# Joining neighbouring filter spectra by accumulating DMA instead of VectorE adds, in a gated mix of a long convolution and a token-mixing MLP

## The chip, the cores and the metric

One core of one Trainium2 chip runs the whole kernel. The metric is device time in microseconds (us). Before the change three runs gave 226.09, 227.66 and 223.95 us; the median is 226.09 us.

## The reference

Sequence length S is 2048, width D is 640, the MLP's hidden width F is 1536, batch 1. Cut to what matters:

```
g = sigmoid((q * gate_w).sum(-1))
k_shift[t] = sum_j k[t - 3 + j] * shift_k[:, j]          # 4 taps, causal
kv = k_shift * v
y  = causal convolution of kv with ssm_k, length S, per column   # rfft/irfft of 2S
a  = q * (y + kv * ssm_D)
h  = layernorm(q);  u = gelu(w1^T h + b1);  b = w2^T u + b2       # mixes tokens
out = g * a + (1 - g) * b
```

## The kernel before

**Engines and their order.** Every operation is handed to a planner (`_Plan`, class at line 322) with an engine, a guessed cost, a priority, and the regions that it reads and writes. The planner simulates the engines and writes out one fixed order for each of PE (matmul), ACT, DVE and POOL and for the two queues that issue transfers, SP and POOL. At run time every engine goes through its list in order; a wait for data or for a buffer holds up all that stands behind it on that engine. PSUM is four slots of 1024 columns (`pp0` to `pp3`).

**The convolution by blocks.** The sequence is cut into P = 4 blocks of 512 rows. Filter block i (`wnat`, transposed on PE into `wT`, its even part split into `ee`) is transformed by matmuls with cosine and sine tables (`TFc`, `TFs`, `TN`) into a spectrum `W0` to `W3` of nine rows of 640 columns on 128 partitions: real parts of four frequency groups f = 0 to 3 (rows 0 to 3), a row 4 for the real part's Nyquist term, and imaginary parts (rows 5 to 8). `w_freq` copies each PSUM tile into `W` on ACT with a scale.

`w_comb(i)` then joins neighbours, from i = 3 down to 1: in groups 2 and 3 `W_i += W_(i-1)`, in groups 0 and 1 `W_i -= W_(i-1)`. `w_nyq(i)` copies row 3 into row 4, then one element row of row 8 into row 4, both by DMA on SP, and zeroes partition 0 of row 8 (`memset`, on POOL). It does this for all four spectra, W0 among them.

**The input blocks.** For block j, four tiles of the key with its four taps (`k4`, 128 x 2560) are loaded by SP, multiplied by the taps on DVE (`k<-k,shkb`), added up over the taps by PE with `ident` or `flip`, copied to `kvb` by ACT, and multiplied by `v` on DVE. A DVE split (`es`) and 32 matmuls with `AFc` and `AFs` give the spectrum `A_j`, copied to SBUF by ACT. There is one `kvb` and one `es` buffer.

**Products and inverses.** For output block m, `pair(j, m)` multiplies `A_j` with `W_(m-j)` on DVE, for j = 0 to m, and adds up into `Z` (two buffers; `tT` is the scratch). `inverse(m)` turns `Z` back by 32 matmuls with the table `TI`; `epilogue` copies the results (`qb`, `pb`), flips by PE, scales by the gate on ACT into `cg`, and combines on DVE with the MLP's result `o` and with `xe`, then stores by SP. For the last m the products are split by frequency group.

**The MLP.** `h` comes from a layernorm on DVE; the first product (`pp<-h,w`, 384 matmuls) and the second (`pp<-gT,w`, 384) fill PE wherever nothing else is ready. Weights come by DMA on POOL's queue (`w1_0` to `w1_2`, `w2_0`, `w2_1`), each load waiting for PE to have done with the old tile. The gate's row sums (`xg`) use DVE and ACT.

Of the kernel before, what the change touches and what calls it, by code (L numbers as in the profile page):

```python
# [8 lines left out]
BF16 = mybir.dt.bfloat16  # L9
F32 = mybir.dt.float32  # L10
I32 = mybir.dt.int32
ACT = mybir.ActivationFunctionType
ALU = mybir.AluOpType
# [4 lines left out]
class _Tracker:  # L18
# [227 lines left out]
    def dma(self, stream, out_ap, in_ap, semname, noncontig=False, accum=False):  # L246
        reads = [in_ap]
        writes = [out_ap]
        acc = self.pre(stream, reads, writes)
        engobj = self.eng[stream]  # L250
        sem = self.dma_sems[semname]
        if accum:
            ins = engobj.dma_start(out_ap, in_ap, accum_op=ALU.add)
        elif noncontig:
            with self.nc.allow_non_contiguous_dma(reason="tiny"):
                ins = engobj.dma_start(out_ap, in_ap)
        else:
            ins = engobj.dma_start(out_ap, in_ap)  # L258
        ins.then_inc(sem, 16)
        self.dma_cnt[semname] += 16  # L260
        v = self.dma_cnt[semname]
        self.dma_hist[(semname, v)] = dict(self.known[stream])
        src = ("dma", semname, v)
        for reg, mode in acc:
            self.add_record(reg, mode, src)
        return v
# [250 lines left out]
def _build(nc, A_q, A_k, A_v, A_shift_k, A_ssm_k, A_ssm_D, B_x, B_w1, B_b1, B_w2, B_b2, gate_w, out):  # L517
    Bsz, S, D = A_q.shape
# [4 lines left out]
    n = S // P  # L523
    N2 = 2 * n
# [4 lines left out]
    HD = D // 2  # L529
# [3 lines left out]
    with ExitStack() as es:  # L533
# [3 lines left out]
        T = _Tracker(nc, clk)  # L537
# [5 lines left out]
        plan = _Plan(T, 4)  # L543
# [4 lines left out]
        def buf(name, shape, dtype, t0, t1):  # L548
            spec.append((name, list(shape), dtype, t0, t1))

        END = 999
# [33 lines left out]
        buf("AFc", [128, 1024], BF16, 0, 90)  # L585
        buf("AFs", [128, 1024], BF16, 0, 90)
        buf("TI", [128, 2, 4, n // 2], BF16, 0, END)
        buf("h", [128, NT, D], BF16, 0, 80)
        groups = [[0], [1]] + [[t, t + 1] for t in range(2, NT, 2)]
        for i in range(2):  # L590
# [50 lines left out]
        for name, shape, dtype, t0, t1 in spec:  # L641
            size = mybir.dt.size(dtype)
# [31 lines left out]
        def tt(out_, in0, in1, op, pr, eng="DVE"):  # L674
            c = 0.07 + nel(out_) / 1920.0 if eng == "DVE" else 0.3 + nel(out_) / 500.0
            return vop(eng, c, lambda e: e.tensor_tensor(out_, in0, in1, op), [in0, in1], [out_], pr)  # L676

        def ts(out_, in0, s1, s2, op0, op1, pr, eng="DVE", cost=None):
            c = cost if cost is not None else (0.1 + nel(out_) / 1500.0 if eng == "DVE" else 0.4 + nel(out_) / 900.0)

            def f(e):
                if s2 is None:
                    return e.tensor_scalar(out_, in0, s1, None, op0=op0)
                return e.tensor_scalar(out_, in0, s1, s2, op0=op0, op1=op1)

            rr = [in0] + [a for a in (s1, s2) if isinstance(a, bass.AP)]
            return vop(eng, c, f, rr, [out_], pr)
# [5 lines left out]
        def memset(ap, val, pr, eng="POOL"):  # L693
            return vop(eng, 0.3 + nel(ap) / 2000.0, lambda e: e.memset(ap, val), [], [ap], pr)

        def act(out_, in_, func, pr, bias=None, scale=None, accum=None, ps=(), after=()):
            kw = {}
            rr = [in_]
            k = 0
            if bias is not None:  # L700
                kw["bias"] = bias
                if isinstance(bias, bass.AP):
                    rr.append(bias)
                    k += 1
            if scale is not None:
                kw["scale"] = scale
                if isinstance(scale, bass.AP):
                    rr.append(scale)
                    k += 1
            ww = [out_]  # L710
            if accum is not None:
                kw["accum_out"] = accum
                ww.append(accum)
            c = 0.17 + nel(out_) / 1150.0 + 0.09 * k + (0.2 if accum is not None else 0)

            def f(e):
                src = in_() if callable(in_) else in_
                return e.activation(out_, src, func, **kw)  # L718

            return vop("ACT", c, f, rr, ww, pr, ps=ps, after=after)  # L720

        def dma(out_ap, in_ap, semname, pr, stream="SP", noncontig=False):
            if semname not in T.dma_sems:
                T.add_dma_sem(semname, es.enter_context(nc.semaphore(f"d_{semname}")))
            tot = mybir.dt.size(out_ap.dtype)
            for st, ct in list(out_ap.ap):
                tot *= ct

            def emit():
                T.dma(stream, out_ap, in_ap, semname, noncontig=noncontig)  # L730

            return plan.add(stream, 1.2 if stream == "POOL" else 0.5, emit, [in_ap], [out_ap], pr, dma=max(tot, 20000) / 1e6)

        def pe(pslist, mms, pr, after=()):
            reads = []
# [11 lines left out]
        def two(p_):  # L747
            return lambda: pp[p_.slot][:, :].rearrange("p (c f) -> p c f", c=2)[:, :, 0:HD]
# [4 lines left out]
        def h2(ap):  # L753
            return ap.rearrange("p (c f) -> p c f", c=2)

        b = bufs
# [11 lines left out]
        c_pi, c_hp, c_mh, c_w, c_w0, c_mn, c_mn2 = (cst[:, i:i + 1] for i in range(7))  # L768
# [42 lines left out]
        TFc, TFs, AFc, AFs, TI = b["TFc"], b["TFs"], b["AFc"], b["AFs"], b["TI"]  # L811
# [72 lines left out]
        for gi, g in enumerate(groups):  # L884
            xs = b[f"xs{g[0] // 8}"][:, g[0] % 8:g[-1] % 8 + 1, :]
            gn = len(g)
            pr = 1.0 + g[0] * 0.08
# [29 lines left out]
        p_ = _PS()  # L917
# [4 lines left out]
        for j in range(KS):  # L922
            p_ = _PS()
# [31 lines left out]
        def w_freq(i, pr):  # L955
            osrc = b[f"wT{i}"]
            W = b[f"W{i}"]
            for fi in ORD:
                for c in range(2):
                    p_ = transform(b[f"ee{i % 2}"], osrc, fi, c, pr)  # L960
                    act(h2(W[:, 5 * c + fi, :]), two(p_), ACT.Copy, 1, scale=c_w if fi == 3 else 2.0 / N2, ps=[p_])

        for i in range(P):
            w_time(i)
# [9 lines left out]
        for gi, g in enumerate(groups):  # L974
            mms = []
# [21 lines left out]

        def w_comb(i, pr):
            W, V = b[f"W{i}"], b[f"W{i - 1}"]


            def half(t, f):
                return bass.AP(tensor=t, offset=f * D, ap=[[9 * D, 128], [5 * D, 2], [1, 2 * D]])

            tt(half(W, 2), half(W, 2), half(V, 2), ALU.add, pr)
            tt(half(W, 0), half(W, 0), half(V, 0), ALU.subtract, pr)

        def w_nyq(i):
            W = b[f"W{i}"]
            dma(W[:, 4, :], W[:, 3, :], f"wn{i}", 17)  # L1010
            dma(W[0:1, 4, :], W[0:1, 8, :], f"wn{i}", 17)
            memset(W[0:1, 8, :], 0.0, 2)

        def kv_load(t, pr):
            nm = f"k4_{t % KR}"
# [27 lines left out]
        def a_freq(j, pr):  # L1043
            A = b[f"A{j}"]
            es_ = b["es0"]
            for fi in ORD:
                for c, tab in ((0, AFc), (1, AFs)):
                    p_ = _PS()
                    e0 = 0 if (fi >= 2) == (c == 0) else 2
                    pairs = [(tf(tab, nb, fi), es_[:, e0 + nb, :]) for nb in range(2)]  # L1050
                    pe([p_], halves(p_, pairs), pr)
                    act(h2(A[:, c, fi, :]), two(p_), ACT.Copy, 1, ps=[p_])

        def kv_two(i):
            for t in range(NB * i, NB * i + NB):
# [52 lines left out]
                act(h2(b[f"o1_{q}"][:, k, :]), two(p_), ACT.Identity, 3, bias=b["c2"][:, sb:sb + 1],  # L1108
                    scale=b["omg"][:, sb:sb + 1], ps=[p_])

        def tabs(c, fi, i):
            return TI[:, c, fi, i * 128:(i + 1) * 128]

        def inverse(m_):
            Z = b[f"Z{m_ % 2}"]
            res = [_PS() for _ in range(4)]
            part = (((0, 2), (0, 3), (1, 0), (1, 1)), ((1, 2), (1, 3), (0, 0), (0, 1)))
            if z_split(m_):
                for i in range(2):
                    for k, fi in enumerate(ORD):  # L1120
                        mms = []
                        for g in range(2):
                            c = [c_ for c_, f_ in part[g] if f_ == fi][0]
                            for h_ in range(2):
                                mms.append((res[2 * i + g], h_ * 512, HD, tabs(c, fi, i),
                                            Z[:, c, fi, h_ * HD:(h_ + 1) * HD], k == 0, k == 3))
                        pe([res[2 * i], res[2 * i + 1]], mms, 1.0)
            else:
                for i in range(2):
                    for g in (1, 0):  # L1130
                        pairs = [(tabs(c, fi, i), Z[:, c, fi, :]) for c, fi in sorted(part[g], key=lambda x: x[1])]
                        pe([res[2 * i + g]], halves(res[2 * i + g], pairs), 1.0)
            return res

# [56 lines left out]
        ts(b["gg"][:, :], b["gth"][:, :], 0.5, 0.5, ALU.mult, ALU.add, 20, eng="POOL")  # L1191
        ts(b["omg"][:, :], b["gth"][:, :], -0.5, 0.5, ALU.mult, ALU.add, 20, eng="POOL")
        tt(b["c2"][:, :], b["omg"][:, :], b["bf"][:, FT:FT + NT], ALU.mult, 20, eng="POOL")
        for q in range(NO):
            mlp2(q)
        for m_ in range(P):
# [37 lines left out]
```

## Time and profile before

| | before |
|---|---|
| median of 3 runs | 226.09 us (223.95 to 227.66) |
| span of the profiled execution | 222.4 us |
| instructions | 3751 |
| DMA moved | 39.88 MB, mean 179 GB/s |
| POOL's queue | 3104 packets, 11.54 MB, 17.9% of 16 engines |
| SP's queue | 18964 packets, 28.10 MB, 39.8% |
| granted TensorE clock | 1.00 in every 10 us stretch but 10 to 20 us (0.83) and the last (0.90) |

The runs' times include some microseconds around the profiled span: the median is 3.7 us longer than it. In the profile's rows a line is that of a helper that records operations (L290 for every matmul, L676 for every tensor-tensor, L718 for every ACT operation, L258 for every DMA), so groups are told apart by tile names, written out<-in. A row of the timeline gives start, busy time, engine, line, operation, tiles, and, in brackets, how long the engine was idle before it and what ended that. A DVE or ACT row's busy time overlaps the next one by some 0.08 us, so the advance from start to start is a little shorter than the busy time. The idle time of an engine that bounds nothing costs nothing.

### The profile page before, as it was taken

Reading aid. Unit: us, or ns where it says so; the run is one execution under the profiler, and the core shown is the slowest. Engines: PE = TensorE matmul, PEld = TensorE weight load, DVE = VectorE, ACT = ScalarE, POOL = GpSimd, SP = SyncE. Lnnn points to the kernel's source line nnn. Section 1 sums busy time; section 2 is a strip of 40 time slices with the busy share of each in tenths; the row PEclk is TensorE's granted clock in tenths of the full one; section 3 lists DMA queues with packets and bytes.
Section 4 is the critical chain, followed back from the end, with each engine's and each line's share of the span. In section 5 each row is a group of like instructions: output and inputs, shape, how many; then the busy total and the mean of one; then the engine's idle time right before and its main releaser. Section 6 shows DMA issues by size and latency. Waiting matters only on the chain.

```text
span 222.4 us, 3751 instructions
## 1 busy us (share of the span) xinstructions
PE 202.8 (91%) x1481; PEld 141.1 (63%) x1481; DVE 201.8 (91%) x253; ACT 139.9 (63%) x221; POOL 41.5 (19%) x79
## 2 busy tenths in 40 slices
PE   0829799999998998999999999999999999999991
PEld 0725547567675774777777777667777777767651
DVE  3379999899988998999999999999999999999771
ACT  4899988997579869683746511799431845432251
POOL 8563330301131010015171010000101101110000
PEclk9988999999999999999999999999999999999997
DMA  6999996139915894899962114302065845286003
GB/s 180 359 325 349 235 298 244 43 109 304 347 41 146 297 391 160 287 295 294 288 181 58 36 16 140 119 3 59 0 202 169 244 116 180 83 253 200 0 3 118
DMA packets 22087, 39.88 MB, mean 179 GB/s; under 512 B 1715, under 2 KB 17205, under 8 KB 22069
## 3 DMA queue, kind: packets, MB, share of 16 engines
q1 hardware_dynamic: 18964, 28.10, 39.8%
q0 software_dynamic: 3104, 11.54, 17.9%
q8 instruction: 12, 0.20, 0.4%
q14 instruction: 7, 0.05, 0.1%
HBM read 36.35 MB, written 2.62 MB: 175 GB/s over the span
## 4 chain that ended last, share of the span: by engine, by line
PE 60%; DVE 22%; ACT 11%; DMA 5%; issue 1%; DVEq 0%; SPq 0%
PE pp L290 60%; DVE Z L676 10%; DVE tT L676 7%; DMA k<-in_A_k_dram 3%; ACT wT L718 2%; ACT W L718 2%; DMA wnat<-in_A_ssm_k_dram 2%; ACT L718 1%; DVE es L676 1%; DVE cg L676 1%; ACT kvb L718 1%; DVE kvb L676 1%; DVE k L676 1%; DVE xg L676 1%; ACT TFs L718 1%
## 5 line engine op out<-in xcount | busy, mean ns | idle before, releaser
L290 PE MATMUL pp<-h,w 128*128 128x320 bf16 x384 | 54.9, 299 | 0.0
L290 PE MATMUL pp<-gT,w 128*128 128x320 bf16 x384 | 53.1, 299 | 0.0
L676 DVE TENSOR_TENSOR tT<-A,W 128x640 bf16<-128x640 bf16 (+4 forms) x44 | 48.0, 1121 | 0.3
L676 DVE TENSOR_TENSOR Z<-Z,tT 128x2560 bf16<-128x2560 bf16 (+3 forms) x35 | 47.1, 1370 | 0.1
L290 PEld LDWEIGHTS pp<-gT,w 128*128 128x128 bf16 x384 | 37.5, 98 | 14.8 <-issue 0.3
L290 PEld LDWEIGHTS pp<-h,w 128*128 128x128 bf16 x384 | 37.5, 98 | 14.6
L258 POOL DMA_DIRECT2D w<-in_B_w_dram x18 | 17.3, 962 | 117.7 <-PE pp L290 117.1
L718 ACT ACTIVATE o<-pp,c,omg 128x640 bf16<-128x640 f32 x16 | 14.2, 884 | 31.4 <-PE pp L290 31.4
L676 DVE TENSOR_TENSOR k<-k,shkb 128x2560 bf16<-128x2560 bf16 x16 | 23.4, 1485 | 0.6 <-DMA k<-in_A_k_dram 0.5
L718 ACT ACTIVATE A<-pp 128x640 bf16<-128x640 f32 x32 | 20.0, 717 | 2.0 <-PE pp L290 2.0
L718 ACT ACTIVATE gT<-pp,bf 128x640 bf16<-128x640 f32 x12 | 9.5, 792 | 18.3 <-PE pp L290 18.2
L290 PE MATMUL pp<-Z,TI 128*128 128x320 bf16 x128 | 18.4, 299 | 1.1 <-ACT kvb L718 1.1
L718 ACT ACTIVATE W<-pp 128x640 bf16<-128x640 f32 x24 | 15.9, 707 | 3.9 <-PE pp L290 3.8
L290 PE MATMUL pp<-ident,wnat 128*128 128x128 bf16 x80 | 8.0, 274 | 10.1 <-DMA wnat<-in_A_ssm_k_dram 5.4
L290 PEld LDWEIGHTS pp<-Z,TI 128*128 128x128 bf16 x128 | 12.4, 98 | 6.4 <-ACT kvb L718 1.4
L718 ACT ACTIVATE kvb<-pp 128x640 bf16<-128x640 f32 x16 | 11.2, 701 | 5.8 <-PE pp L290 5.8
L290 PEld LDWEIGHTS pp<-ident,wnat 128*128 128x128 bf16 x80 | 6.6, 124 | 11.2 <-DMA wnat<-in_A_ssm_k_dram 5.8
L893 DVE BATCH_NORM_STATS2 stats<-xs 128x6 f32<-128x320 bf16 x32 | 13.3, 475 | 0.0
L718 ACT ACTIVATE xg<-xg 128x640 bf16<-128x640 bf16 x16 | 11.6, 734 | 1.7 <-DVE xg L676 1.7
L676 DVE TENSOR_TENSOR Z<-A,W 128x5120 bf16<-128x5120 bf16 x4 | 11.3, 2819 | 0.7 <-ACT A L718 0.7
L290 PE MATMUL pp<-wT,TFc 128*128 128x320 bf16 x48 | 10.1, 300 | 1.7 <-ACT W L718 1.7
L290 PE MATMUL pp<-es,AFs 128*128 128x320 bf16 x64 | 10.1, 300 | 0.8 <-ACT gT L718 0.8
(92 smaller groups left out, 279.2 us busy)
## 6 DMA issues: line engine op xcount, KB each, us to landing
k<-in_A_k_dram SPq DMA_DIRECT2D x15, 640.0 KB, 7.7
w<-in_B_w_dram POOLq DMA_DIRECT2D x8, 768.0 KB, 5.8
w<-in_B_w_dram POOLq DMA_DIRECT2D x10, 512.0 KB, 6.1
wnat<-in_A_ssm_k_dram SPq DMA_DIRECT2D x4, 640.0 KB, 6.5
v<-in_A_v_dram SPq DMA_DIRECT2D x16, 160.0 KB, 7.4
xg<-in_A_q_dram SPq DMA_DIRECT2D x8, 320.0 KB, 7.1
xe<-in_A_q_dram SPq DMA_DIRECT2D x8, 320.0 KB, 3.1
out_dram<-cg SPq DMA_DIRECT2D x8, 320.0 KB, 4.3
```

The lines of the kernel that those rows point to most:

```text
L258: ins = engobj.dma_start(out_ap, in_ap)
L290: ins = self.nc.tensor.matmul(ps_ap, lhsT=lhsT, rhs=rhs, start=start, stop=stop)
L676: return vop(eng, c, lambda e: e.tensor_tensor(out_, in0, in1, op), [in0, in1], [out_], pr)
L718: return e.activation(out_, src, func, **kw)
L893: vop("DVE", 0.41, (lambda o_, i_: lambda e: e.bn_stats(o_, i_))(o_, i_), [i_], [o_], pr)
```

## The change

The DVE adds and subtracts of `w_comb` go. In their place two transfers for each i (real and imaginary rows, 128 x 2 x 1280 elements, 655 KB each) add `W_(i-1)` to `W_i` within SBUF, issued on POOL's queue with an accumulating add. Since a transfer can only add, the sign goes elsewhere: for odd blocks the groups f = 0 and 1 of `W` (scale in `w_freq`) and of `A` (scale in `a_freq`) are stored negated, and the inverses of odd m read a negated copy of the table for these groups, `TIn`, made by one POOL operation. The zeroing of row 8 moves from POOL to DVE. In the planner the accumulating transfers are given 2.5 times the size, and all orders are planned anew.

```diff
         if accum:
-            ins = engobj.dma_start(out_ap, in_ap, accum_op=ALU.add)
+            ins = engobj.dma_start(out_ap, in_ap, accum_op=ALU.add, max_dma_last_dim=2560)
...
+        buf("TIn", [128, 2, 2, n // 2], BF16, 84, END)
...
+            size = max(tot, 20000) / 1e6 * (2.5 if accum else 1.0)
+            return plan.add(stream, 1.2 if stream == "POOL" else 0.5, emit, [in_ap], [out_ap], pr, dma=size)
...
-                    act(h2(W[:, 5 * c + fi, :]), two(p_), ACT.Copy, 1, scale=c_w if fi == 3 else 2.0 / N2, ps=[p_])
+                    sc = c_w if fi == 3 else (-2.0 / N2 if fi < 2 and i % 2 else 2.0 / N2)
+                    act(h2(W[:, 5 * c + fi, :]), two(p_), ACT.Copy, 1, scale=sc, ps=[p_])
...
         def w_comb(i, pr):
             W, V = b[f"W{i}"], b[f"W{i - 1}"]
-            def half(t, f):
-                return bass.AP(tensor=t, offset=f * D, ap=[[9 * D, 128], [5 * D, 2], [1, 2 * D]])
-
-            tt(half(W, 2), half(W, 2), half(V, 2), ALU.add, pr)
-            tt(half(W, 0), half(W, 0), half(V, 0), ALU.subtract, pr)
+            for c in range(2):
+                dma(W[:, 5 * c:5 * c + 4, :].rearrange("p (u f) d -> p u (f d)", u=2),
+                    V[:, 5 * c:5 * c + 4, :].rearrange("p (u f) d -> p u (f d)", u=2),
+                    f"wj{i}_{c}", pr, stream="POOL", accum=True)
...
-            memset(W[0:1, 8, :], 0.0, 2)
+            memset(W[0:1, 8, :], 0.0, 2, eng="DVE")
...
-                    act(h2(A[:, c, fi, :]), two(p_), ACT.Copy, 1, ps=[p_])
+                    sc = {"scale": -1.0} if fi < 2 and j % 2 else {}
+                    act(h2(A[:, c, fi, :]), two(p_), ACT.Copy, 1, ps=[p_], **sc)
...
-        def tabs(c, fi, i):
-            return TI[:, c, fi, i * 128:(i + 1) * 128]
+        def tabs(c, fi, i, m_):
+            t = b["TIn"] if fi < 2 and m_ % 2 else TI
+            return t[:, c, fi, i * 128:(i + 1) * 128]
...
+        ts(b["TIn"][:, :, :, :], TI[:, :, 0:2, :], -1.0, None, ALU.mult, None, 6, eng="POOL")
```

The parts left out pass `m_` to `tabs` and `accum` through the kernel's `dma` helper.

More of the change, by code (lines that the diff above doesn't have):

```diff
@@ L720, in act, with dma @@
             return vop("ACT", c, f, rr, ww, pr, ps=ps, after=after)
-        def dma(out_ap, in_ap, semname, pr, stream="SP", noncontig=False):
+        def dma(out_ap, in_ap, semname, pr, stream="SP", noncontig=False, accum=False):
             if semname not in T.dma_sems:
@@ L729, in emit @@
             def emit():
-                T.dma(stream, out_ap, in_ap, semname, noncontig=noncontig)
-            return plan.add(stream, 1.2 if stream == "POOL" else 0.5, emit, [in_ap], [out_ap], pr, dma=max(tot, 20000) / 1e6)
+                T.dma(stream, out_ap, in_ap, semname, noncontig=noncontig, accum=accum)
+            size = max(tot, 20000) / 1e6 * (2.5 if accum else 1.0)
+            return plan.add(stream, 1.2 if stream == "POOL" else 0.5, emit, [in_ap], [out_ap], pr, dma=size)
         def pe(pslist, mms, pr, after=()):
@@ L1124, in inverse @@
                             for h_ in range(2):
-                                mms.append((res[2 * i + g], h_ * 512, HD, tabs(c, fi, i),
+                                mms.append((res[2 * i + g], h_ * 512, HD, tabs(c, fi, i, m_),
                                             Z[:, c, fi, h_ * HD:(h_ + 1) * HD], k == 0, k == 3))
@@ L1130, in inverse @@
                     for g in (1, 0):
-                        pairs = [(tabs(c, fi, i), Z[:, c, fi, :]) for c, fi in sorted(part[g], key=lambda x: x[1])]
+                        pairs = [(tabs(c, fi, i, m_), Z[:, c, fi, :]) for c, fi in sorted(part[g], key=lambda x: x[1])]
                         pe([res[2 * i + g]], halves(res[2 * i + g], pairs), 1.0)
```

## The prediction

> **What bounds the kernel now.** I read the page first, then the busy time by stage, then the DVE, PE and POOL timelines around the first filter products.
>
> ```profile
> span 222.4 us, 3751 instructions
> PE 202.8 (91%) x1481; PEld 141.1 (63%) x1481; DVE 201.8 (91%) x253; ACT 139.9 (63%) x221; POOL 41.5 (19%) x79
> ...
> PE 60%; DVE 22%; ACT 11%; DMA 5%; issue 1%; DVEq 0%; SPq 0%
> ```
>
> Two engines are full at once, and the chain of waits passes between them.
>
> ```profile
> 60.00:80.00 20.00, 19.22 (x142) 13.51 (x140) 18.23 (x18) 17.15 (x31) 3.09 (x5) 1.00 0.61 193
> 80.00:100.00 20.00, 18.86 (x138) 12.81 (x137) 18.97 (x19) 15.63 (x30) 1.32 (x2) 1.00 0.81 270
> 100.00:210.00 110.00, 109.70 (x806) 77.99 (x805) 109.47 (x102) 53.14 (x78) 15.92 (x16) 1.00 0.45 134
> ```
>
> Columns: stretch, length, busy PE, PEld, DVE, ACT, POOL, clock, DMA share, GB/s. From 100 to 210 us DVE and PE each idle half a microsecond. DVE work that slips past 100 us therefore has no room before the end.
>
> ```profile
> 97.69 1.56 DVE L676 TENSOR_TENSOR es<-kvb 128x1280 bf16<-128x1280 bf16 x2
> 99.17 1.48 DVE L676 TENSOR_TENSOR k<-k,shkb 128x2560 bf16<-128x2560 bf16 x1
> ...
> 209.11 0.88 DVE L676 TENSOR_TENSOR Z<-Z,tT 128x640 bf16<-128x640 bf16 x2
> ```
>
> DVE ends the input split of block 2 (es) at 99.17 and the last product sum (Z) at 209.99: 110.8 us between them, then 12.4 us of last inverse, output and store.
>
> ```profile
> 85.61 2.33 PE L290 MATMUL pp<-k,ident 128*128 128x320 bf16 x16
> 89.08 2.33 PE L290 MATMUL pp<-Z,TI 128*128 128x320 bf16 x16 [1.14 <-ACT kvb L718]
> 91.25 2.34 PE L290 MATMUL pp<-k,flip 128*128 128x320 bf16 x16
> 93.42 0.43 PE L290 MATMUL pp<-v,flip 128*128 128x320 bf16 x2
> 93.69 2.34 PE L290 MATMUL pp<-h,w 128*128 128x320 bf16 x16
> 95.87 0.43 PE L290 MATMUL pp<-v,flip 128*128 128x320 bf16 x2
> ```
>
> These are block 2's tap products on PE; 16 matmuls advance PE by 2.17 us, 0.136 each.
>
> **What is removed.** `w_comb`: the W<-W group is x6, 8.9 us, all of it on DVE between 47.5 and 70.8 us. Four small memsets come to DVE; none is in the trace, so they lie between its 0.15 us one-column operation and its 0.48 us 640-wide one. I take 0.3 each, 1.2. Net relief: 7.7 us. The sign edits (an ACT scale, another table in an inverse) cost nothing: they are operands of instructions that run already.
>
> **What is moved.** Zeroing row 0 of W0 must now follow the last accumulating transfer, since that one reads W0. In the built order the first full product, Z<-A0,W0, comes behind this memset, and so behind the input work of blocks 1 and 2, xg included. In the trace before it starts at 63.3 us. Only a 1920-wide and a 640-wide product of it stay early. DVE can thus not fill its waits for block 1 and 2 tiles with products: the relief becomes idle time.
>
> When does block 2's split end now? PE works in order. Up to block 1's first tap product (69.59 us before) it now also holds 16 more weight matmuls (+2.2) and loses some of its small idles (1.51, 0.29, 0.39 and 0.78 us): I keep 69.5. Then, ahead of and with block 2's taps, stand 36 tap and flip matmuls of block 1, 16 weight, 16 es, 16 weight, 8 es, 16 weight, 8 es, 32 weight, 36 of block 2: 184 x 0.136 = 25.0, plus 0.8 for es of block 1 (ready at 77.4): 95.3 us. In the trace the last v flip ends at 96.30 and es starts at 97.69, 1.4 later; so es runs 96.7 to 98.2, one xg (0.74) follows, and the memset stands at 98.9.
>
> From there to the last Z, by the built order, with the advance that the DVE timeline gives each width (5120: 2.74, 2560: 1.40, 1920: 1.07, 1280: 0.74, 640: 0.40): 3 memsets 0.9; 14 of 5120, 38.4, five of them 0.12 longer for their wait, 0.6; 31 of 2560, 43.4; 8 of 1920, 8.6; 14 of 640, 5.6; 19 of 1280, 14.1; the split last pair 12.4 (196.85 to 209.99, less one cg). Sum 124.0. The same count over 102.98 to 209.99 before gives 105.9 where the trace has 107.0, so I add 1.1: 125.1, against 110.8 before.
>
> A new wait: block 3's split overwrites es, which PE reads until 188 matmuls (25.5 us) after the first inverse can start; DVE gets there 20.5 us after releasing that inverse. DVE stands 5 us, and behind it wait all the products of m=1 to 3. PE may also be up to 2 us late with block 3's first tap. I take 5 of 0 to 7.
>
> Last Z: 98.9 + 125.1 + 5 = 229.0. No weight product is left behind the last inverse, so the tail is 8 matmuls 1.2, two pb copies 1.55, flips 0.8, cg 0.8 on ACT, three 0.74 steps of cg on DVE 2.3, store 2.6 (219.78 to 222.4): 9.2. Span 238.2. The median of the runs, 226.09, is 3.7 over the profiled span; with that, 241.9, call it 242.
>
> **The transfers.** Six of 655 KB on POOL's queue, chained: W2's own sum starts when W3's has read it, W1's after that. No accumulating transfer is in the trace. Lower bound: the 512 KB w load of the same queue, 6.1 us to landing. Upper: 160 KB within SBUF took 7.9 and 1.2 KB 2.8, so four times the bytes 2.8 + 4.1 x 5.1 = 24. I take 10, nearer to the row of the same queue, since the destination is read as well. The first two go out near 50 us (W3 complete on ACT). The last waits on POOL behind a w load that needs PE to have done its old tile (85.0 us): 85.0 + 0.9 + 1.0 = 87, landing at 97, under the 98.9 at which DVE arrives. It is hidden by 2 us; beyond 12 us it is added one for one. POOL's w loads wait behind the sums' waits; with 10 us each they land 7 us or more before PE asks. On SP the copies of the Nyquist row wait for the sums with the next k loads behind them; those k loads wait for PE longer.
>
> The Trainium skill ("Collectives: The Full Stack", section "The bandwidth ceiling") says that a reduction by DMA runs at half a copy's rate because it reads two sources, not because of the add. By it an estimate is twice 7.6 us (6.1 scaled to 655 KB), 15, and the sum would be 245 (87 + 15 is 3 past 98.9); no run yet shows it.
>
> The negated table TIn is one POOL instruction of 1024 columns: by POOL's 128-column flipn (0.57) and 2-column vpe (0.29) 2.8 us, in POOL's wait at about 125 us, needed by PE at 144: hidden.
>
> ```profile
> 113.03 0.50 POOL L684 TENSOR_SCALAR gg<-gth 128x16 f32<-128x16 f32 x1
> 113.50 0.19 POOL L684 TENSOR_SCALAR omg<-gth 128x16 f32<-128x16 f32 x1
> 113.78 2.67 POOL L676 TENSOR_TENSOR c<-omg,bf 128x16 f32<-128x16 f32 x1
> ```
>
> A 16-column operation took 2.67 us while DVE's 2.87 us product ran (113.50 to 116.37): POOL waited, DVE did not. The Trainium skill ("SBUF — State Buffer", "Who interferes with whom") says that a DVE instruction with two SBUF inputs and a GpSimd one that reads exclude each other, whoever comes first. By it DVE could stand the 2.8 us instead, and the sum would be 245; the row above is the other order of the same rule.
>
> **Rivals.**
> 1. Relief wins (other side). DVE meets that memset early: the old end, 210, less 125.1 puts the deciding point at 85 us. Then PE alone bounds: its end 217.9 less up to 5 us of mid idles, and a 5 to 8 us tail without filler: span 218 to 224, time 222 to 228, just over 2% faster at best. For it: 7.7 us less DVE work. Against: 112 weight and es matmuls (15.2 us) stand ahead of block 2's taps. Chance 0.11, of which 0.03 faster by over 2%.
> 2. Slow transfers. From 12 us to landing the last sum holds W0's memset, and through shared queues the k loads at 50 to 60 us, a stretch where DMA is 0.98 busy. At 24 us: +12, 254; with k late too, 260. Chance 0.17.
> 3. The sums never overlap work and starve PE of w tiles: needs the first to land after 72 us (w due at 78.4), so over 20 us; the same side as 2 and within its price.
>
> **Numbers.** Forecast 242, chance 0.72; without the es wait and with es 2 us earlier 235, with 7 us and a last transfer of 15 us 247. For 8 in 10 I take 232 to 256: this, the upper half of rival 2, a little of rival 1. The runs before spread from 223.95 to 227.66, so 2% (4.5 us) is about what can be told. Faster 0.03, same 0.09, slower 0.88.
>
> **What would show it.** DVE at 58 to 98 us with 15 us or more of idle, ended by ACT kvb; the first 5120-wide Z near 99 us, not 63; DVE's last Z 15 to 22 us later than 210; PE idle ahead of the last inverse. Wrong if Z starts before 85 us, if DVE's wait ends by a wj transfer well past 99 us (rival 2), or if PE is full to the end (rival 1).

## The result, and the profile after

| | before | after |
|---|---|---|
| median, same chip | 225.09 us (223.95 to 227.66, 4 runs) | 252.16 us (251.58 to 253.88, 4 runs) |
| span of the profiled execution | 222.4 us | 250.3 us |
| DVE idle from 40 to 140 us | 3.9 us | 36.2 us |
| end of the last Z on DVE | 210.0 us | 240.1 us |

The ratio is 1.1203, 95% interval [1.1126, 1.1279]: the change makes the kernel 12% slower. Here and below a median counts every run, while a ratio and its interval leave out the runs that took over 1.5% longer than the fastest one of the same kernel. The page of the changed kernel, first its head and then the chain that ended last:

```profile
span 250.3 us, 3756 instructions
PE 211.5 (85%) x1481; PEld 143.5 (57%) x1481; DVE 196.9 (79%) x251; ACT 141.1 (56%) x221; POOL 49.0 (20%) x82
...
PE 48%; DVE 33%; ACT 9%; DMA 4%; issue 4%; DVEq 0%
```

DVE is busy 4.9 us less and PE has the same 1481 matmuls, yet neither is full any more. The busy time by stretch (columns as before) says where:

```profile
60.00:80.00 20.00, 17.79 (x125) 11.42 (x124) 7.54 (x8) 15.17 (x28) 3.81 (x6) 1.00 1.06 297
80.00:100.00 20.00, 17.85 (x128) 11.93 (x126) 9.33 (x12) 11.56 (x21) 5.20 (x5) 1.00 1.06 323
100.00:120.00 20.00, 18.26 (x134) 12.74 (x131) 16.28 (x17) 10.75 (x19) 3.22 (x4) 1.00 0.89 303
120.00:140.00 20.00, 19.44 (x142) 13.78 (x143) 16.12 (x19) 9.82 (x19) 4.80 (x6) 1.00 0.40 116
```

DVE idles 23.1 us between 60 and 100 us and 7.6 us between 100 and 140. The DMA share, as the view counts it, is past 1.00 for 40 us. The whole loss is in DVE's books: its idle time grows by 32.3 us from 40 to 140 us, by 1.1 before and 1.4 after; less the 4.9 us by which its busy time fell that is 29.9 us, against 30.1 us by which the last Z came later. DVE's timeline, at the places that the prediction names and at one that is used further down:

```profile
97.78 0.49 DVE L677 TENSOR_TENSOR kvb<-kvb,v 128x640 bf16<-128x640 bf16 x1 [9.33 <-ACT kvb L719]
...
105.01 1.56 DVE L677 TENSOR_TENSOR es<-kvb 128x1280 bf16<-128x1280 bf16 x2
...
107.31 0.33 DVE L695 MEMSET W<- 1x320 uint32 x1
107.67 2.83 DVE L677 TENSOR_TENSOR Z<-A,W 128x5120 bf16<-128x5120 bf16 x1
...
150.90 3.73 DVE L677 TENSOR_TENSOR Z<-Z,tT 128x2560 bf16<-128x2560 bf16 x2
...
239.22 0.89 DVE L677 TENSOR_TENSOR Z<-Z,tT 128x640 bf16<-128x640 bf16 x2
```

The first 5120-wide product stands at 107.7 us. Before, it stood at 63.3:

```profile
63.34 2.82 DVE L676 TENSOR_TENSOR Z<-A,W 128x5120 bf16<-128x5120 bf16 x1 [0.75 <-ACT A L718]
```

What DVE waits for is the input path. Between 58 and 98 us its idle time is 22.8 us: 15.0 us of it is ended by ACT (9.3 by the copy of a tap sum, kvb, which ACT can make only when PE has formed the sum), and 7.8 us by loads of k. PE's timeline in the same stretch, and at the end:

```profile
88.09 2.34 PE L290 MATMUL pp<-h,w 128*128 128x320 bf16 x16
90.26 1.25 PE L290 MATMUL pp<-es,AFs 128*128 128x320 bf16 x8
91.35 4.51 PE L290 MATMUL pp<-h,w 128*128 128x320 bf16 x32
95.70 2.34 PE L290 MATMUL pp<-k,ident 128*128 128x320 bf16 x16
99.73 1.26 PE L290 MATMUL pp<-k,flip 128*128 128x320 bf16 x8 [1.69 <-DVE k L677]
...
103.23 13.20 PE L290 MATMUL pp<-h,w 128*128 128x320 bf16 x96
116.27 1.25 PE L290 MATMUL pp<-k,ident 128*128 128x320 bf16 x8
...
233.14 2.31 PE L290 MATMUL pp<-Z,TIn 128*128 128x320 bf16 x8 [12.50 <-DVE Z L677]
```

While DVE stands 9.3 us for kvb (88.4 to 97.8), PE runs 48 weight products of the MLP ahead of block 2's taps (95.70). Between the taps of block 2 and of block 3 (116.27) it runs another 96, 13.2 us in one piece. PE is busy with work that nobody is waiting for yet, and the taps stand behind it. That work is then missing at the end, where PE stands 12.5 us for DVE. In the built order 281, 429, 577 and 709 matmuls stand ahead of the first taps of blocks 0 to 3; before the change it was 249, 413, 529 and 629.

### The profile page after: what moved, and what is told of

Read it like the earlier page. It is cut to its first block, busy times and chain, and to the rows that moved or that the text cites. A ratio compares the mean times of both kernels' runs of the same rounds, so it can differ in the third digit from the quotient of the medians.

```text
span 250.3 us, 3756 instructions
## 1 busy us (share of the span) xinstructions
PE 211.5 (85%) x1481; PEld 143.5 (57%) x1481; DVE 196.9 (79%) x251; ACT 141.1 (56%) x221; POOL 49.0 (20%) x82
## 4 chain that ended last, share of the span: by engine, by line
PE 48%; DVE 33%; ACT 9%; DMA 4%; issue 4%; DVEq 0%
PE pp L290 48%; DVE Z L677 14%; DVE tT L677 13%; DVE cg L677 5%; ACT wT L719 2%; DMA out_dram<-cg 2%; DMA wnat<-in_A_ssm_k_dram 2%; ACT kvb L719 1%; ACT A L719 1%; DVE k L677 1%; ACT L719 1%; ACT W L719 1%; ACT cg L719 1%; ACT TFs L719 1%; ACT TFc L719 0%
## 5 line engine op out<-in xcount | busy, mean ns | idle before, releaser
L677 DVE TENSOR_TENSOR Z<-Z,tT 128x2560 bf16<-128x2560 bf16 (+3 forms) x35 | 48.0, 1394 | 0.1
L719 ACT ACTIVATE A<-pp 128x640 bf16<-128x640 f32 x32 | 20.8, 707 | 9.1 <-PE pp L290 8.9
L677 DVE TENSOR_TENSOR kvb<-kvb,v 128x640 bf16<-128x640 bf16 x16 | 7.7, 489 | 18.6 <-ACT kvb L719 12.1
L290 PE MATMUL pp<-Z,TIn 128*128 128x320 bf16 x32 | 8.1, 385 | 14.4 <-DVE Z L677 14.4
L719 ACT ACTIVATE qb<-pp 128x640 bf16<-128x640 f32 x8 | 5.6, 704 | 23.5 <-PE pp L290 23.5
L719 ACT ACTIVATE W<-pp 128x640 bf16<-128x640 f32 x24 | 16.6, 703 | 3.7 <-PE pp L290 3.6
L719 ACT ACTIVATE kvb<-pp 128x640 bf16<-128x640 f32 x16 | 11.3, 704 | 11.5 <-PE pp L290 11.1
L290 PE MATMUL pp<-Z,TI 128*128 128x320 bf16 x96 | 16.8, 323 | 0.3 <-issue 0.3
L290 PEld LDWEIGHTS pp<-Z,TIn 128*128 128x128 bf16 x32 | 3.6, 119 | 17.5 <-DVE Z L677 14.2
L895 DVE BATCH_NORM_STATS2 stats<-xs 128x6 f32<-128x320 bf16 x32 | 13.4, 476 | 0.0
L290 PEld LDWEIGHTS pp<-ident,wnat 128*128 128x128 bf16 x80 | 7.4, 136 | 10.5 <-DMA wnat<-in_A_ssm_k_dram 5.4
L290 PEld LDWEIGHTS pp<-Z,TI 128*128 128x128 bf16 x96 | 9.9, 105 | 5.8 <-issue 0.6
## 6 DMA issues: line engine op xcount, KB each, us to landing
k<-in_A_k_dram SPq DMA_DIRECT2D x15, 640.0 KB, 12.8
W<-W POOLq DMA_DIRECT2D x6, 640.0 KB, 12.8
xg<-in_A_q_dram SPq DMA_DIRECT2D x8, 320.0 KB, 11.1
```

Of the source, the lines that this page charges most:

```text
L290: ins = self.nc.tensor.matmul(ps_ap, lhsT=lhsT, rhs=rhs, start=start, stop=stop)
L895: vop("DVE", 0.41, (lambda o_, i_: lambda e: e.bn_stats(o_, i_))(o_, i_), [i_], [o_], pr)
```

## The experiments

The median of the kernel before, run beside each group, lay between 225.4 and 226.2 us. Every ratio is against it.

### The parts of the change, one at a time

The first run keeps everything of the change but the transfers: the signs, `TIn` and the memsets on DVE stay, and the joins are DVE adds.

```diff
-            for c in range(2):
-                dma(W[:, 5 * c:5 * c + 4, :]..., V[:, 5 * c:5 * c + 4, :]..., f"wj{i}_{c}", pr, stream="POOL", accum=True)
+            for f in (0, 2):
+                hw = bass.AP(tensor=W, offset=f * D, ap=[[9 * D, 128], [5 * D, 2], [1, 2 * D]])
+                hv = bass.AP(tensor=V, offset=f * D, ap=[[9 * D, 128], [5 * D, 2], [1, 2 * D]])
+                tt(hw, hw, hv, ALU.add, pr)
```

> The joins are VectorE adds again (six of 2560 columns, 8.9 us), but the alternating signs, the negated table TIn and the memsets on DVE stay. Theory A (the time went because the transfers that add leave the first products late in DVE's order, and its waits empty): near the kernel before, 222 to 229 us. Rival C (signs, table or memsets on DVE cost the time): 240 us or more. Rival B (the transfers themselves are slow or crowd the queues) says the same as A here.

Measured: 227.53 us (224.64 to 230.43, 10 runs), ratio 1.0037 [0.9989, 1.0084]. Signs, table and memsets together cost nothing that can be told; all of the loss belongs to the transfers and what they entail.

The second keeps the changed kernel's order and waits and issues each sum for 256 of its 1280 columns (131 KB for 655; the other columns are not joined).

```diff
+                if accum:
+                    T.dma(stream, out_ap[:, :, 0:256], in_ap[:, :, 0:256], ..., accum=accum)
+                    return
                 T.dma(stream, out_ap, in_ap, semname, noncontig=noncontig, accum=accum)
```

> The order of every engine and all waits of the changed kernel, but each accumulating transfer moves 256 of 1280 columns a row (131 KB, not 655): most of the joining is left out. Theory A: the order alone makes it slow; only the crowding of the k loads goes, so block 2's split ends near 98 to 101 instead of 106.5 us and the time is 244 to 249 us. Rival B (slow transfers): 226 to 234 us. If B had no part at all: 252.

Measured: 252.74 us (252.02 to 254.57), ratio 1.1154 [1.1064, 1.1245]. Four fifths of the bytes away, and no gain: theory A missed, and what came is the 252 us for the case that the bytes have no part at all. The DMA issues (size, median to landing) of the changed kernel:

```profile
k<-in_A_k_dram SPq DMA_DIRECT2D x15, 640.0 KB, 12.8
...
W<-W POOLq DMA_DIRECT2D x6, 640.0 KB, 12.8
```

Those of the run with small sums, and two rows of its DVE timeline:

```profile
k<-in_A_k_dram SPq DMA_DIRECT2D x15, 640.0 KB, 7.1
...
W<-W POOLq DMA_DIRECT2D x6, 128.0 KB, 6.7
```

```profile
74.28 1.56 DVE L677 TENSOR_TENSOR tT<-A,W 128x1920 bf16<-128x1920 bf16 x2 [10.53 <-ACT A L719]
...
107.56 0.33 DVE L695 MEMSET W<- 1x320 uint32 x1
```

The key loads land in 7.1 us, where the changed kernel has 12.8, and DVE no longer waits for them; it waits 10.53 us for ACT's A instead, and the memset of W0 stands at 107.56, as before. In this order the transfers' bytes are covered by PE's own lateness.

The third and fourth take away the hazard on which the prediction was built. In one, row 8 of W0 is not zeroed; in the other it is saved to a row of its own first, so that W0 can be zeroed early, and added to W1 by DVE.

```diff
-            memset(W[0:1, 8, :], 0.0, 2, eng="DVE")
+            if i:
+                memset(W[0:1, 8, :], 0.0, 2, eng="DVE")
```

```diff
+        copy(nq, b["W0"][0:1, 8, :], 2, "DVE")
+        w_nyq(0)
         w_comb(1, 17.0)
-        for i in range(P):
+        tt(b["W1"][0:1, 8, :], b["W1"][0:1, 8, :], nq, ALU.add, 2)
+        for i in range(1, P):
             w_nyq(i)
```

> Full transfers, but partition 0 of W0's row 8 is not zeroed (left out), so the first product need not follow the last transfer; planned anew. Theory A: the first 5120-wide Z goes back to 62 to 75 us and some 7 us of products of block 0 fall into DVE's waits; 242 to 246 us. Rival B: unchanged, 250 to 254 us.

> The same release without leaving work out: W0's row 8 of partition 0 is copied to a small tile and zeroed early, and added to W1 by a DVE operation of one partition after the last transfer. Theory A: as with the row not zeroed, plus about 1 us for the two small operations; 242 to 247 us. Rival B: 250 to 255 us.

Measured: 252.80 us, ratio 1.1159 [1.1057, 1.1261], and 253.12 us, 1.1175 [1.1074, 1.1276]. Theory A missed in both; the times are those of rival B, unchanged. The busy time by stretch of the kernel that does not zero W0:

```profile
60.00:100.00 40.00, 35.88 (x253) 23.50 (x251) 22.29 (x22) 26.35 (x46) 8.21 (x8) 1.00 1.05 304
100.00:140.00 40.00, 37.31 (x271) 26.24 (x272) 25.02 (x30) 19.32 (x36) 6.15 (x9) 1.00 0.65 210
```

The first product did move, to 69.9 us, and DVE did 5.4 us more by 100 us (22.29 against 16.87). But from 100 to 140 it did 7.4 us less (25.02 against 32.40): the products were used up, and the input of blocks 2 and 3 was no earlier (es of block 2 at 105.67). Moving products forward only moved the idle time back. In this order the lateness of the input path is what sets the end.

### The planned order

New theory: the order. The planner is told that an accumulating transfer takes 2.5 times its bytes. By its model of the DMA rate that is some 5.5 us for each of six in series, so loads behind them look late, and it fills PE with weight products first. One number is changed, and nothing else:

```diff
-            size = max(tot, 20000) / 1e6 * (2.5 if accum else 1.0)
+            size = max(tot, 20000) / 1e6 * (0.2 if accum else 1.0)
```

(1.0 and 5.0 in the next two; the last has 0.2 and the saved row.) In these expectations blocks are counted from one: their blocks 3 and 4 are blocks 2 and 3 elsewhere.

> The changed kernel with one number of the planner altered: an accumulating transfer is charged 0.2 of its size in the model, not 2.5 times (2.5 puts about 5.5 us of DMA time on each of the six, in series, so that loads behind them look late and weight matmuls are planned ahead of the input taps). The work and the transfers are the same; the planned order differs: ahead of the first tap product of block 3 stand 545 matmuls, not 577, of block 4 645, not 709, and the first full product stands at row 69 of DVE's order, not 86. Theory A (the planned order is what costs): 226 to 236 us, DVE busy 17 us or more in each 20 us stretch from 60 to 140. Theory B (the order is a consequence of the chain of transfers and stays late on the chip whatever the model charges): 248 us or more. Theory C (transfers land at 12.8 us each, and an order that trusts them to be fast stalls on them): above 240 us, DVE or PE idle ended by a transfer of W.

> The same with a charge of 1.0 times the size, as a plain transfer. Planned order between: 561 matmuls ahead of block 3's first tap, 677 ahead of block 4's, and the first full product late. Theory A: 236 to 248 us, between the kernel with 0.2 and the changed one. Theory B: 250 us or more. Theory C: no slower than with 0.2.

> The same with a charge of 5.0 times the size: the counts ahead of the taps are those of the changed kernel (429, 577, 709), but the first inverse comes another 88 matmuls (12 us) later, at 825. Theory A: 255 to 265 us. Theory B: 250 to 254 us, as the changed kernel.

> A charge of 0.2 and, besides, W0's row 8 saved to a row of its own, so that W0 can be zeroed before the transfers are done (the row is added to W1's by DVE). 545 matmuls ahead of block 3's taps, the first inverse at 569. Theory A: 224 to 233 us, 1 to 3 us below the kernel with 0.2 alone, since the one wait of W0 on the last transfer is gone. Theory B: 248 us or more. Theory C: 236 us or more, a wait ended by a transfer of W1 to W3.

| charge | median | ratio | first taps of blocks 1, 2, 3 on PE |
|---|---|---|---|
| 0.2 | 244.71 us | 1.0822 [1.0740, 1.0903] | 88.0, 102.8, 116.4 |
| 1.0 | 244.58 us | 1.0827 [1.0742, 1.0913] | 72.4, 100.2, 116.0 |
| 2.5 (the change) | 252.16 us | 1.1203 [1.1126, 1.1279] | 74.2, 95.7, 116.3 |
| 5.0 | 257.30 us | 1.1418 [1.1328, 1.1508] | 74.3, 97.1, 116.5 |
| 0.2, row saved | 241.48 us | 1.0682 [1.0599, 1.0765] | 89.2, 102.8, 118.4 |

The same work and the same transfers give 244.7 to 257.3 us, by the planner's guess alone; B falls. A holds for 5.0: the first taps stand as in the change, and the first inverse on PE starts at 135.6 us, not 122.1. For 1.0 the time lies in A's range, but level with 0.2 and not above it, as theory C had it. With 0.2 A fell short: it asked for 226 to 236, and for 224 to 233 with the row saved. The row saved gains 3.2 us there, at the edge of what the intervals can tell; in the order of the change it gained nothing.

With 0.2 the steps from block 1 to 2 to 3 are now short (14.8 and 13.6 us, where the change has 21.6 and 20.6), and the delay sits ahead of block 1. PE's timeline there, and the busy time by stretch, for the charge of 0.2:

```profile
69.33 1.31 PE L290 MATMUL pp<-es,AFs 128*128 128x320 bf16 x8 [0.20 <-ACT A L719]
82.22 4.45 PE L290 MATMUL pp<-h,w 128*128 128x320 bf16 x16 [11.59 <-DMA w<-in_B_w_dram]
86.46 1.71 PE L290 MATMUL pp<-es,AFs 128*128 128x320 bf16 x8
88.01 2.34 PE L290 MATMUL pp<-k,ident 128*128 128x320 bf16 x16
```

```profile
60.00:80.00 20.00, 9.16 (x65) 5.73 (x62) 4.48 (x3) 8.74 (x16) 5.73 (x7) 0.84 1.07 283
```

PE stands 11.59 us for a weight load. This order trusts the transfers to be quick, and now their cost comes out. That is theory C in its time, but only in part in its sign: of DVE's waits between 55 and 100 us, 4.4 us end by a transfer of W, and 11.1 and 7.9 us by loads of k and xg. With the charge of 1.0 the same cost shows elsewhere: PE does not stand for a weight load, but a load of xg that went out at 62.9 us took 22.8 us to land, and the chain that ended last runs through it.

### The bytes, in the better order

If the transfers cost nothing in the slow order because PE was later still, they should cost their full price in the good one. The next run puts the cut of the second experiment (256 of 1280 columns) into the kernel with the charge of 0.2, order unchanged.

> The kernel with the charge of 0.2, its order unchanged, with each accumulating transfer cut to 256 of its 1280 columns a half (131 KB in place of 655; the rest of the sums is left out). In the trace of the kernel with 0.2, DVE stands 28 us between 60 and 100 us for loads of k and xg and for transfers of W; SP stands 25 us in that stretch for sums, with those loads queued behind. Theory D (in this order the sums' transfers are late, and hold SP's queue): 228 to 236 us, SP's waits for W under 12 us in all. Theory E (what is left is PE's order and the zeroing of W0 behind the chain, whatever the bytes): 241 to 246 us.

Measured: 231.28 us (227.68 to 234.34), ratio 1.0188 [1.0048, 1.0328]. D holds; whether this kernel is 2% slower than the one before stays open. The profiled execution is the longest of the four (234.34 us); its busy time by stretch and the row at which PE had stood:

```profile
60.00:100.00 40.00, 38.11 (x278) 26.59 (x277) 31.42 (x34) 32.03 (x61) 7.51 (x9) 1.00 0.93 300
```

```profile
72.78 2.35 PE L290 MATMUL pp<-h,w 128*128 128x320 bf16 x16 [0.42 <-DMA w<-in_B_w_dram]
```

The wait is 0.42 us, and taps of blocks 1 to 3 start at 76.1, 89.6 and 103.2 us. So the two causes cover each other:

| | order of the change (2.5) | order with 0.2 |
|---|---|---|
| sums of 655 KB | 252.16 us | 244.71 us |
| sums of 131 KB | 252.74 us | 231.28 us |

Undoing the bytes alone brings nothing, undoing the order alone 7.5 us, both together 20.9 us of the 24.6 us between the change and the kernel with signs only. In the order with 0.2 the bytes are worth 13.4 us by the medians (14 us by the ratios).

Do the bytes cost through a queue (loads that stand behind a sum's wait) or through the DMA engines themselves? Three runs move work between queues, with the bytes unchanged and the orders planned anew: the eight copies of the Nyquist rows go from SP, where k, v and xg are loaded, to POOL, without and with the saved row; then the later weight loads of the first product go from POOL, behind the sums, to SP as well.

```diff
-            dma(W[:, 4, :], W[:, 3, :], f"wn{i}", 17)
-            dma(W[0:1, 4, :], W[0:1, 8, :], f"wn{i}", 17)
+            dma(W[:, 4, :], W[:, 3, :], f"wn{i}", 17, stream="POOL")
+            dma(W[0:1, 4, :], W[0:1, 8, :], f"wn{i}", 17, stream="POOL")
...
-                        ..., stream="SP" if s_ < 1 else "POOL")
+                        ..., stream="SP")
```

> The kernel with the charge of 0.2, with the eight copies of the Nyquist rows issued from POOL, where the sums are issued, in place of SP, where the loads of k, v and xg are queued behind their waits. Bytes and work are the same. Theory D1 (SP's queue is held by those copies): 229 to 237 us, no wait of DVE for k or xg over 3 us between 60 and 100. Theory D2 (the transfers crowd the 16 DMA engines, and the queue matters little): 241 to 246 us. Rival: weight loads on POOL come late behind the copies and PE waits for w: 240 us or more, with PE idle ended by a load of w.

> Charge of 0.2, the copies on POOL, and W0's row 8 saved, so that W0 is zeroed before the sums. Theory D1: 225 to 234 us, 2 to 4 below the one without the saved row. Theory D2: 239 to 245 us.

> As the kernel with the charge of 0.2 and the row copies on POOL (243.66 us), with the 512 KB weight loads of the second and later sets issued from SP, so that no load at all stands behind a sum in a queue. There, PE stood 12.4 us for a weight load that POOL issued at 72.5, behind four sums. Theory D1 (the queue behind the sums is what costs): 229 to 236 us, PE's wait for w below 4 us. Theory D2 (the DMA engines are full from 60 to 80 us, with the sums' 3.9 MB among the loads, and whichever load comes later is late, from any queue): 239 to 245 us, DVE or PE idle 15 us or more from 60 to 85 us, ended by loads.

Measured: 243.66 us (ratio 1.0826 [1.0736, 1.0917]), 241.96 us (1.0751 [1.0656, 1.0846]) and 244.00 us (1.0743 [1.0647, 1.0840]). All three lie in D2's range and none in D1's; the rival of the first holds as well, since PE stood 12.4 us for a weight load. Waits of DVE and PE between 55 and 100 us (total, times, longest), with the copies on POOL and then with the weight loads on SP as well:

```profile
DVE xg L677 <- DMA xg<-in_A_q_dram: 4.3, 2, 3.4
...
PE pp L290 <- DMA w<-in_B_w_dram: 12.4, 1, 12.4
```

```profile
DVE k L677 <- DMA k<-in_A_k_dram: 9.1, 4, 4.0
DVE xg L677 <- DMA xg<-in_A_q_dram: 8.6, 1, 8.6
DVE W L695 <- DMA W<-W: 5.4, 2, 3.2
...
PE pp L290 <- DMA w<-in_B_w_dram: 7.4, 1, 7.4
```

In the last run no load that is late stands behind a sum, and it is late all the same: the weight load that PE waits for went out on SP at 63.0 us and took 15.3 us to land, the one of xg at 63.8 us and took 19.0. DMA is 1.08 busy at 281 GB/s from 60 to 80 us. Four fifths of six sums are 3.15 MB; at the 283 GB/s of the kernel with 0.2 an estimate is 11.1 us of full DMA time, near the 13.4 us between the two kernels. The Trainium skill ("DMA: Bandwidth & Descriptors", section "Issuing engines are not separate DMA queues") says that transfers started by different engines run on the same 16 DMA engines and interleave there; these runs agree.

But crowding is not shown to be the whole price. With 0.2, the weight load that PE waited for went out 4.7 us later than with small sums (70.8 against 66.1 us), behind the sums on POOL, and then took 4.8 us longer to land (11.4 against 6.7): about half of that delay was the queue's. In the last run, where that queue is out of the way, the chain that ended last runs through the sums themselves, one after the other. The second link took 12.8 us and the third 9.9; two copies of rows follow, and DVE's memset waits for them until 94.2 us. How the 13.4 us divide between loads that land late, loads behind a sum and the chained sums stays open.

No version beats the kernel before. Sums that go out at another time of the kernel, where DMA is idle (0.17 busy from 140 to 160 us before), were not tried: the products need the joined spectra earlier. The 3.75 us that are left between the small sums (231.28) and signs only (227.53) were not taken apart; in the profiled executions DVE's idle time from 40 to 140 us is 14.3 us there and 3.1 us with signs only, which is 3.5 us more than the 7.7 us of relief.

## Why the prediction was right, and where it was not

The side and the range were right: 252.16 us lies in 232 to 256 and 10 us over the forecast. So was half of the mechanism: PE in order, with the taps behind weight products, DVE idle for want of them, and the last Z late. The other half, the zeroing of W0 as the step that decides, was not the cause. That the number came out in the range in spite of this is partly luck. Step by step:

- **Signs, table, memsets: nothing.** Shown by the first run. A memset took 0.33 us, taken at 0.3. `TIn` took 2.78 us on POOL, taken at 2.8. It was not quite hidden in the run with signs only, where it took 3.4 us and PE stood 1.5 us for it, without a difference in time that can be told.
- **Relief becomes idle time.** Right in kind, too small in size. DVE idles from 58 to 98 us as the prediction said, though only 9.3 of its 22.8 us are ended by kvb. The first full product is late (107.7 us, where it said near 99), and PE stands ahead of the last inverse. The last Z came 30.1 us later than before, not 15 to 22.
- **Block 2's split at 96.7 us, memset at 98.9.** The largest miss: 105.01 and 107.31, 8.4 us later. The prediction's count of matmuls was that of the order, but it let PE run without gaps. Block 1's first tap came at 74.15 instead of 69.5 (block 0's taps were already late, 50.74 against 45.77 before), which accounts for most of the rest. From block 2's first tap to its split 9.3 us passed where the prediction has 6.3, 3.0 us of the 8.4: there PE waited 1.69 us for DVE's k product, because that stands behind a kvb product that waits for ACT.
- **Zeroing W0 as the step that decides.** (The prediction calls it row 0; it is partition 0 of row 8.) Wrong as a cause, though right as a place in the order. With that hazard gone, the products come at 69.9 us and the time stays at 252.8. What failed is the sentence that DVE "can thus not fill its waits": once the hazard was gone it filled them and had nothing left 40 us later. The order of PE and the transfers' bytes stood behind both.
- **Memset to last Z, 125.1 us and 5 us of waiting for es.** Measured 132.8 us (107.3 to 240.1), 2.7 more than the two together. The es wait was 0.36 us, because DVE came to that split 25.5 us after the first inverse had begun and not 20.5; the idle time was spread over other tiles, 7.6 us from 100 to 140.
- **The tail, 9.2 us.** Measured 10.2 (240.1 to 250.3). The three misses, 8.4, 2.7 and 1.0, are the 12.1 us between spans of 238.2 and 250.3. The time around the span was 1.9 us, taken at 3.7. Where a run lists both figures they lie 1.7 to 2.8 us apart, so the median of three was set against the span of one of the faster runs.
- **Transfers of 10 us, hidden by 2 us.** Median 12.8 us to landing. The last was issued at 91.9 instead of 87 and landed 10.0 us later, at 101.9, and the memset of W0 at 107.31 did not wait: hidden in this order, by 5.4 us. But the reason was half the truth. They were hidden because PE was late, and they cost 13.4 us in the order in which it is not. Rival 2 saw the price (k loads late in a full DMA) in an order in which it is not paid; rival 3, PE starved for w, is what the kernel with the charge of 0.2 does, for 11.59 us.
- **Relief wins (rival 1).** Ruled out: even with a fifth of the bytes and the better order, 231.28 us are above the kernel before (ratio 1.0188, from 1.0048 up).

Two rules of the Trainium skill were weighed. The half rate ("Collectives: The Full Stack", section "The bandwidth ceiling"), told there of a collective, would have given 15 us a sum and 245 us in all; landing took 12.8 us, between that and the 10 us taken. POOL's queue, with the 3.93 MB of the sums more, took 24.0% of 250.3 us against 17.9% of 222.4: 20.3 us of all 16 engines, 194 GB/s, where its other 11.54 MB went at 290 GB/s. As an estimate, if those other bytes took no longer than before, that is 0.67 of a load's rate in a crowded stretch; the direction agrees, the half was not reached.

The port rule (the Trainium skill, "SBUF — State Buffer", section "Who interferes with whom") would have had DVE stand the whole 2.8 us of `TIn`. The POOL row beside DVE's row at 150.90:

```profile
150.84 2.78 POOL L684 TENSOR_SCALAR TIn<-TI 128x1024 bf16<-128x1024 bf16 x1 [16.86 <-PE pp L290]
```

DVE's two sums took 3.73 us there. The same two elsewhere:

```profile
224.79 2.89 DVE L677 TENSOR_TENSOR Z<-Z,tT 128x2560 bf16<-128x2560 bf16 x2
```

So 0.84 us were lost, not 2.8; here the measurement decides.

## What to carry to other kernels

Where two engines are full, work that was taken from one and given to the DMA was paid for where the DMA engines were full; add up the bytes that the stretch already moves before calling a transfer hidden. A planner's guess for a new kind of operation moves everything else too: here the guess alone was worth 12.6 us between 0.2 and 5.0. And when an experiment that removes a suspected cost changes nothing, remove a second one with it: bytes and order covered each other, and neither test alone showed the 13.4 us.

## What the hardware showed unasked

**An idle PE comes back slow.** After 12.5 us of waiting, 8 matmuls took 2.31 us where 8 in a busy stretch take 1.25, and the granted clock of the last full stretch was 0.50:

```profile
230.00:240.00 10.00, 6.07 (x22) 2.94 (x23) 10.00 (x22) 0.00 (x0) 0.00 (x0) 0.50 0.00 0
```

With the charge of 0.2, 16 matmuls after the wait of 11.59 us took 4.45 us instead of 2.34. The Trainium skill ("TensorE: Matmul & The Clock Gate", "HAM oscillation — how this bites in real kernels") says that gaps of PE of more than some 3.4 us return it to the slow clock. These rows agree: the starved PE paid 2 us more than its wait.

**A fifth of the bytes does not land in a fifth of the time.** In the order of the change the small sums took 6.7 us to landing against 12.8. POOL was held 1.2 us for the issue of each, small or large.
